# LayerNorm outputs of six token groups turned to channel rows by a DRAM write and a transposing DMA load in place of TensorE

## The chip, the cores and the metric

One core of a Trainium2 chip runs the whole program. The metric is the device time of one execution in microseconds (us), lower is better. TensorE is the matrix engine (PE, with PEld for its weight loads), VectorE is DVE, ScalarE is ACT, GpSimd is POOL, SyncE is SP. SBUF is the core's on-chip memory, in which most of the kernel's buffers lie in one piece, `arena`. PSUM is the memory that TensorE's results go to; its tiles here are `ph` (first product), `po` (second product) and `pt` (transposes). DRAM lies outside the core.

## The reference, cut to what matters

Two kinds of layer alternate, twice. A is a gated long convolution, B is a channel MLP. `x` is 2048 tokens of 512 channels, in bfloat16.

```python
x = A_q
x = x + _A_ref(_layernorm(x), A_k, A_v, ...)   # = x + layernorm(x) * y ; y depends on k and v only
x = x + _B_ref(_layernorm(x), w1, b1, w2, b2)
x = x + _A_ref(_layernorm(x), A_k, A_v, ...)   # the same y
x = x + _B_ref(_layernorm(x), w1, b1, w2, b2)

def _B_ref(x, w1, b1, w2, b2):
    y = _layernorm(x)
    h = _gelu(y @ w1 + b1)          # 512 -> 1376
    return h @ w2 + b2              # 1376 -> 512
```

The kernel computes `y` once, in its first part (up to about 118 us). The second part, the MLP part, works on groups of 512 tokens: four groups of layer 1 (numbers 0 to 3) and four of layer 2 (4 to 7). The LayerNorm of a group leaves tokens on partitions. The first matrix product needs channels on partitions, so the LayerNorm's output must be transposed: 512 x 512 elements, 512 KB, which is 16 blocks of 128 x 128.

## The kernel before: the parts that matter

```python
GT, CT, FT = 4, 4, 11       # token tiles of a group, channel tiles, hidden tiles
lnT = [place(f"lnT{i}", [P, CT, GT * P], ...) for i in range(2)]   # channel rows
lnx = [place(f"lnx{i}", [P, GT, D], ...) for i in range(2)]        # token rows

def prep(g):                           # VectorE, with a power step on GpSimd
    ln = lnx[n % 2]
    layernorm(LN[2 + n % 2], ln, g)    # x = x + layernorm(x) * y
    nc.vector.tensor_tensor(tmpa[:], ln[:], YA[...], ALU.mult)
    nc.vector.tensor_tensor(xg, xg, tmpa[:], ALU.add)
    layernorm(LN[n % 2], ln, g)        # the MLP's own LayerNorm
    return n

# PSUM: ps2 has 3 buffers for ph and 3 for po, ps3 has 2 for pt
def ln_transpose(n):                                    # TensorE, then ScalarE
    ln, lt = lnx[n % 2], lnT[n % 2]
    for i in range(GT):
        pt = ps3.tile([P, CT, P], BF16, tag="pt")
        for ct in range(CT):
            nc.tensor.transpose(pt[:, ct, :], ln[:, i, ct * P:(ct + 1) * P], IDt[:])
        nc.scalar.activation(lt[:, :, i * P:(i + 1) * P], pt[:], AF.Copy)

def mm1(n): ...    # first product, 11 x 4 matmuls into ph, gelu on ScalarE into hT
def mm2(n, g, last, between=None):                      # second product
    for i in range(GT):
        if i == GT - 1 and between is not None:
            between()                                   # the next group's transposes
        ...        # 11 matmuls into po, VectorE adds po to x; layer 2 stores x

for i, (l, g) in enumerate(seq):
    mm1(ns[i])
    nxt = None
    if 0 < i < len(seq) - 1:
        ns[i + 1] = prep(seq[i + 1][1])
        nxt = lambda n=ns[i + 1]: ln_transpose(n)
    if i == 0:
        ln_transpose(1)
    if prev is not None:
        mm2(ns[prev], seq[prev][1], seq[prev][0] == 1, nxt)
    prev = i
```

The order of the text is not the order on an engine: the program's scheduler orders each engine's instructions by what depends on what. Only the first part has a hand-written order.

## Time and profile before

| | before |
|---|---|
| time, median of 3 runs | 285.94 us (285.75 to 286.86) |
| span of the profiled run | 283.2 us (that run took 284.89 us, quicker than every other run of this kernel on record, 285.16 us and up) |
| PE, DVE, ACT, POOL busy | 93%, 66%, 59%, 13% of the span |
| mean granted TensorE clock | 0.992 |

The share of the span hides the stages, so the windows view is read first. Its columns are the window, its length, then the busy time with the count of instructions of TensorE, its weight loads, VectorE, ScalarE and GpSimd, the granted clock, the DMA engines' busy share and GB/s. This is a middle window of the MLP part of the kernel before:

```profile
150.00:170.00 20.00, 19.91 (x105) 9.51 (x104) 14.51 (x34) 9.72 (x15) 2.41 (x4) 1.00 0.00 1
```

TensorE is busy 19.91 of 20 us at full clock. ScalarE and VectorE have slack, and the DMA engines stand still. What TensorE does is what counts.

The chain of waits in order of time (start, duration, what) shows what it does in one group of the kernel before:

```profile
150.11 9.50 PE ph L611 x44
159.61 7.13 PE po L623 x33
166.74 0.24 PE pt L602 x4
167.06 0.61 ACT arena L603
167.71 0.38 PE pt L602 x4
168.09 0.22 PE po L623
168.31 0.27 PE pt L602 x4
168.58 1.73 PE po L623 x8
170.31 9.50 PE ph L611 x44
```

From one first product to the next are 170.31 − 150.11 = 20.20 us. The 44 matmuls of the first product take 9.50 us, 0.216 us each. Those of the second take as long (44 x 0.216). The remaining 1.20 us belong to the transposes (pt). A ScalarE copy (ACT arena L603, 0.61 us) stands on the chain between the transposes.

The groups view gives engine, operation, count, busy time and mean ns of one. These are the kernel before's ScalarE copies and transposes:

```profile
L603 ACT ACTIVATE arena<-pt 128x512 bf16<-128x512 bf16 x28 | 15.2, 594 | 38.4 <-PE pt L602 38.2
L602 PE MATMUL pt<-IDt,arena 128*128 128x128 bf16 x112 | 9.6, 218 | 0.5
```

Seven groups are transposed here: 7 x 16 = 112 transposes, 7 x 4 = 28 copies.

### The profile page before, as it was taken

How to read it: one execution, taken by the hardware profiler on the slowest of the kernel's cores; microseconds unless marked ns; L12 is line 12 of the kernel's file. 1: busy time of each engine (PE TensorE's matmuls, PEld its weight loads, DVE VectorE, ACT ScalarE, POOL GpSimd, SP SyncE). 2: the span in 40 equal slices, each digit the busy share in tenths (PEclk: the TensorE clock that was granted, in tenths of full speed). 3: DMA queues.
4: the chain of work that ended last, by engine and by line, in shares of the span. 5: the costliest groups of instructions: out<-in, count | busy, mean ns of one | idle time of the engine just before them, and what ended most of it. 6: DMA issues, size and time to landing. Idle time of an engine off the chain costs nothing.

```text
span 283.2 us, 5560 instructions
## 1 busy us (share of the span) xinstructions
PE 262.8 (93%) x2304; PEld 173.4 (61%) x2304; DVE 187.1 (66%) x346; ACT 167.1 (59%) x210; POOL 36.1 (13%) x67
## 2 busy tenths in 40 slices
PE   3999999999998973779999999999999999999995
PEld 3999999998997973435444444454454454444442
DVE  0989578889999999987565767767767510210221
ACT  1586646779899798887835536437247157067000
POOL 3670000000005103311101101101101100000000
PEclk9999999999999999799999999999999999999999
DMA  7993607994300380000000000000000010110111
GB/s 233 350 420 102 264 2 164 211 216 140 169 2 0 110 293 0 3 1 0 0 2 0 1 0 2 1 0 2 0 0 0 21 56 0 39 38 0 39 56 56
DMA packets 7821, 21.20 MB, mean 75 GB/s; under 512 B 1298, under 2 KB 5108, under 8 KB 6644
## 3 DMA queue, kind: packets, MB, share of 16 engines
q1 hardware_dynamic: 7042, 20.78, 23.1%
q8 instruction: 18, 0.29, 0.4%
q10 hardware_dynamic: 674, 0.07, 0.2%
q0 software_dynamic: 80, 0.00, 0.1%
q14 instruction: 7, 0.06, 0.1%
HBM read 14.56 MB, written 2.10 MB: 59 GB/s over the span
## 4 chain that ended last, share of the span: by engine, by line
PE 79%; DVE 13%; ACT 4%; issue 2%; DMA 1%; POOL 0%; ACTq 0%; DVEq 0%
PE ph L611 26%; PE po L623 26%; PE p_119 L417 3%; PE pt L602 2%; PE p_118 L340 2%; DVE lst_106 L241 2%; DVE T_96 L455 2%; PE p_119 L340 1%; DMA arena<-in_A_ssm_k_dram 1%; PE p_117 L340 1%; PE p_120 L323 1%; ACT arena L603 1%; PE p_118 L417 1%; PE p_117 L323 1%; PE p_118 L323 1%
## 5 line engine op out<-in xcount | busy, mean ns | idle before, releaser
L623 PE MATMUL po<-arena 128*128 128x512 bf16 (+1 forms) x352 | 80.7, 379 | 0.0
L611 PE MATMUL ph<-arena 128*128 128x512 bf16 (+1 forms) x352 | 78.1, 381 | 1.7 <-ACT arena L613 1.7
L613 ACT ACTIVATE arena<-ph,B_74 128x512 bf16<-128x512 f32 (+1 forms) x88 | 60.2, 687 | 26.7 <-PE ph L611 26.7
L611 PEld LDWEIGHTS <-arena 128*128 128x128 bf16 (+1 forms) x352 | 35.4, 101 | 43.1 <-issue 2.8
L626 DVE TENSOR_TENSOR arena<-po,arena 128x512 bf16<-128x512 f32 x32 | 22.0, 687 | 59.0 <-PE po L623 59.0
L623 PEld LDWEIGHTS <-arena 128*128 128x128 bf16 (+1 forms) x352 | 33.8, 98 | 37.4
L603 ACT ACTIVATE arena<-pt 128x512 bf16<-128x512 bf16 x28 | 15.2, 594 | 38.4 <-PE pt L602 38.2
L417 PEld LDWEIGHTS <-arena 128*128 128x128 bf16 x256 | 15.0, 98 | 0.2
L223 ACT ACTIVATE arena<-p_118 128x1024 bf16<-128x1024 f32 (+1 forms) x8 | 10.0, 1247 | 6.5 <-PE p_118 L377 4.7
L323 PEld LDWEIGHTS <-arena 128*128 128x128 bf16 x128 | 11.9, 99 | 1.9 <-issue 0.4
L225 DVE COPY arena<-p_117 128x2048 bf16<-128x2048 bf16 x6 | 7.3, 1220 | 8.0 <-PE p_117 L363 6.9
L489 PEld LDWEIGHTS <-GPt 128*128 128x128 bf16 x128 | 8.3, 104 | 6.4 <-issue 3.7
L602 PEld LDWEIGHTS <-arena 128*128 128x128 bf16 x112 | 8.0, 97 | 6.1 <-issue 3.6
L241 DVE BATCH_NORM_STATS2 lst_106<-arena 128x6 f32<-128x512 bf16 (+2 forms) x20 | 11.2, 578 | 0.3
L225 DVE COPY arena<-p_119 128x2048 bf16<-128x2048 bf16 (+1 forms) x9 | 10.4, 1159 | 1.0 <-PE p_119 L511 0.6
L241 DVE BATCH_NORM_STATS2 lst_110<-arena 128x6 f32<-128x512 bf16 x16 | 10.8, 687 | 0.3
L223 ACT ACTIVATE arena<-p_119 128x1024 bf16<-128x1024 f32 (+3 forms) x8 | 9.5, 1190 | 2.4 <-PE p_119 L377 1.8
L250 POOL TENSOR_TENSOR lrs_108<-lrs_108,mhalf 128x4 f32<-128x4 f32 (+1 forms) x5 | 4.8, 967 | 41.9 <-DVE lnm_109 L247 41.9
L602 PE MATMUL pt<-IDt,arena 128*128 128x128 bf16 x112 | 9.6, 218 | 0.5
L241 DVE BATCH_NORM_STATS2 lst_102<-arena 128x6 f32<-128x512 bf16 x16 | 9.9, 680 | 0.1
L241 DVE BATCH_NORM_STATS2 lst_98<-arena 128x6 f32<-128x512 bf16 x16 | 9.9, 679 | 0.1
L394 POOL TENSOR_SCALAR DG<-IDt,sF 128x128 bf16<-128x128 bf16 x16 | 9.3, 598 | 0.1
(158 smaller groups left out, 404.9 us busy)
## 6 DMA issues: line engine op xcount, KB each, us to landing
arena<-arena SPq DMA_DIRECT2D x8, 512.0 KB, 8.1
arena<-in_A_ssm_k_dram SPq DMA_DIRECT2D x4, 512.0 KB, 4.9
arena<-in_A_k_dram SPq DMA_DIRECT2D x4, 512.0 KB, 6.2
arena<-in_A_v_dram SPq DMA_DIRECT2D x2, 1024.0 KB, 9.5
arena<-tabM SPq DMA_DIRECT2D x1, 2048.0 KB, 7.6
arena<-in_A_q_dram SPq DMA_DIRECT2D x1, 2048.0 KB, 7.9
out_dram<-arena SPq DMA_DIRECT2D x16, 128.0 KB, 1.7
arena<-in_B_w_dram SPq DMA_DIRECT2D x1, 1376.0 KB
```

The costliest lines, as they stand in the source:

```text
L223: nc.scalar.activation(dst, src, AF.Copy)
L225: nc.vector.tensor_copy(dst, src)
L241: nc.vector.bn_stats(self.st[:, i, h, :], x_t[:, GT * g + i, c0:c9])
L323: nc.tensor.matmul(o[:, i, :], src[:, 4 * q + i, cs], Ft[:].rearrange("p x m -> p (x m)"), start=True, stop=True)
L340: nc.tensor.transpose(o[:, i, :], zk, IDt[:])
L417: nc.tensor.matmul(o[:, i, :], w, DG[:, cc, t, :], start=t == 0, stop=t == KS - 1)
L602: nc.tensor.transpose(pt[:, ct, :], ln[:, i, ct * P:(ct + 1) * P], IDt[:])
L603: nc.scalar.activation(lt[:, :, i * P:(i + 1) * P], pt[:], AF.Copy)
L611: nc.tensor.matmul(ph[0:m, :], W1t[:, ct, ft * P:ft * P + m], lt[:, ct, :], start=ct == 0, stop=ct == CT - 1)
L613: nc.scalar.activation(ht[0:m, ft, :], ph[0:m, :], AF.Gelu_apprx_tanh, bias=B1[0:m, ft:ft + 1])
L623: nc.tensor.matmul(po[:], ht[0:m, ft, i * P:(i + 1) * P], W2t[0:m, ft, :], start=ft == 0, stop=ft == FT - 1)
L626: nc.vector.tensor_tensor(xs, po[:], xs, ALU.add)
```

## The change

The 16 transposes and 4 copies of each of the groups 2 to 7 go. Instead GpSimd's queue writes the LayerNorm's output to DRAM, and SyncE's queue loads it back with a DMA that transposes on the way. Such a path is long, so LayerNorms are written two groups ahead, with three buffers in place of two. Group 1 keeps its TensorE transposes.

The diff is cut. Left out are the move of one scratch tile, an unused pool, and index changes.

```diff
+    dram = ctx.enter_context(tc.tile_pool(name="dram", bufs=1, space=bass.MemoryType.DRAM))
...
-    lnT = [place(f"lnT{i}", [P, CT, GT * P], (54 + 4 * i) * K) for i in range(2)]
-    lnx = [place(f"lnx{i}", [P, GT, D], (96 + 4 * i) * K) for i in range(2)]
+    lnT = [place(f"lnT{i}", [P, CT, GT * P], off * K) for i, off in enumerate((54, 58, 86))]
+    lnx = [place(f"lnx{i}", [P, GT, D], (96 + 4 * i) * K) for i in range(3)]
+    lnd = [dram.tile([GT * P, D], BF16, name=f"lnd{i}") for i in range(3)]
...
         layernorm(LN[n % 2], ln, g)
+        nc.gpsimd.dma_start(lnd[n % 3][:, :].rearrange("(i p) d -> p i d", p=P), ln[:])
+        nc.sync.dma_start_transpose(lnT[n % 3][:], lnd[n % 3][:, :])
         return n
...
-        def mm2(n, g, last, between=None):
+        def mm2(n, g, last):
...
-            nxt = None
-            if 0 < i < len(seq) - 1:
-                ns[i + 1] = prep(seq[i + 1][1])
-                nxt = lambda n=ns[i + 1]: ln_transpose(n)
+            if i < len(seq) - 2:
+                ns[i + 2] = prep(seq[i + 2][1])
```

More of the change, by code (lines that the diff above doesn't have):

```diff
@@ L148 @@
     const = ctx.enter_context(tc.tile_pool(name="const", bufs=1))
-    rot = ctx.enter_context(tc.tile_pool(name="rot", bufs=2))
+    dram = ctx.enter_context(tc.tile_pool(name="dram", bufs=1, space=bass.MemoryType.DRAM))
     ROW = 149 * K // 2
@@ L268 @@
     KSW = place("KSW", [P, 2, NA, D // 2], 64 * K)
-    lnT = [place(f"lnT{i}", [P, CT, GT * P], (54 + 4 * i) * K) for i in range(2)]
-    lnx = [place(f"lnx{i}", [P, GT, D], (96 + 4 * i) * K) for i in range(2)]
-    tmpa = place("tmpa", [P, GT, D], 104 * K)
+    lnT = [place(f"lnT{i}", [P, CT, GT * P], off * K) for i, off in enumerate((54, 58, 86))]
+    lnx = [place(f"lnx{i}", [P, GT, D], (96 + 4 * i) * K) for i in range(3)]
+    tmpa = place("tmpa", [P, GT, D], 108 * K)
+    lnd = [dram.tile([GT * P, D], BF16, name=f"lnd{i}") for i in range(3)]
     V2 = place("V2", [P, 2, NA, D // 2], 0)
@@ L285, in prep @@
         xg = x_t[:, GT * g:GT * g + GT, :]
-        ln = lnx[n % 2]
+        ln = lnx[n % 3]
         layernorm(LN[2 + n % 2], ln, g)
@@ L597, in ln_transpose @@
         def ln_transpose(n):
-            ln, lt = lnx[n % 2], lnT[n % 2]
+            ln, lt = lnx[n], lnT[n]
             for i in range(GT):
@@ L605, in mm1 @@
         def mm1(n):
-            lt, ht = lnT[n % 2], hT[n % 2]
+            lt, ht = lnT[n % 3], hT[n % 2]
             for ft in range(FT):
@@ L613, in mm1 @@
                 nc.scalar.activation(ht[0:m, ft, :], ph[0:m, :], AF.Gelu_apprx_tanh, bias=B1[0:m, ft:ft + 1])
-        def mm2(n, g, last, between=None):
+        def mm2(n, g, last):
             ht = hT[n % 2]
             for i in range(GT):
-                if i == GT - 1 and between is not None:
-                    between()
                 po = ps2.tile([P, D], F32, name="po", tag="po")
@@ L643 @@
             if prev is not None:
-                mm2(ns[prev], seq[prev][1], seq[prev][0] == 1, nxt)
+                mm2(ns[prev], seq[prev][1], seq[prev][0] == 1)
             prev = i
```

## The prediction

> **What bounds the kernel now.** The profiled span is 283.2 us (286 us timed). In its second half, from 118 us, TensorE is the limit. The windows view gives it 19.91 of every 20 us busy from 130 to 250 us at granted clock 1.00; ScalarE has 9.7 and VectorE at most 14.5 of 20. In the chain of waits a middle group is 20.20 us long (150.11, 170.31, 190.52, 210.72, 230.92, 251.12: the starts of the first matrix product): 44 matmuls of 0.216 us (9.50 us), 44 of the second product (9.50 us), and 1.20 us for the 16 transposes of the next group's LayerNorm output. The chain shows "PE pt" at 2.3% and the ScalarE copy of that PSUM tile at 1%; the first half (conv, to 118 us) is not touched.
>
> **Removed.** 96 transposes and 24 ScalarE copies (0.594 us each, 14 us in all). ScalarE has slack, so the copies are worth nothing by themselves. On the chain the gain is about 1.20 us for each of six groups: 7.2 us, 2.5% of the run. The transposes of group 1 stay.
>
> **Added.** Six 512 KB writes to DRAM from GpSimd's queue, six 512 KB transposing loads on SyncE's queue; the DMA engines are almost idle there (0 to 1 tenths from 120 us). A 128 KB store lands in 1.7 us here, a 512 KB load in 4.9 to 6.2 us. For the crossbar no duration stands in this trace. The Trainium skill, "DMA: Bandwidth & Descriptors", section "Latency and other measured facts", gives 261 GB/s with a non-contiguous middle dimension, hence an estimate of 2 us plus a fixed cost of about 2 us for 512 KB. I expect about 4 us of write and 4 to 8 us of load, 8 to 12 us in all.
>
> **Moved, and the slack.** LayerNorms already run ahead on VectorE: the second LayerNorm of group 2 ends at 128.5 us (VectorE timeline), while its product would start at 131.85 + 9.50 + 7.56 = 148.9 us. That leaves 20 us. Group 3: ends 139.7, needed 167.9, 28 us. From group 4 on the LayerNorm can start when the second product of four groups earlier is added; it takes about 13 us, and is needed two periods of 19 us later: about 25 us of slack. So all transfers should be hidden and the third buffers avoid waits for reuse. GpSimd's descriptor work may delay the next LayerNorm's power step by 1 to 2 us, which VectorE can absorb.
>
> **Sum.** 285.9 − 7.2 = 278.7 us; I add 0.2 us for small waits between VectorE's additions and the three shared PSUM buffers: 278.9 us. Range (8 in 10): 277.9 to 282.5. Faster by over 2% (under 280.3): 0.78; within 2%: 0.17; slower: 0.05.
>
> **What would show it.** Chain: the starts of the first product 19.0 to 19.1 us apart instead of 20.2; "PE pt" down to one group's 16 transposes; "ACT arena" copies x4. Groups: transposes x16. TensorE idle before the first product: none put down to a DMA. DMA issues: transposing load under 10 us to landing; write under 5 us. Tail after the last addition unchanged (3.5 us).
>
> **What would make it wrong.** (1) A slow crossbar: "VectorE: DVE Perf Modes", section "The three transpose paths", gives 1309 ns for one 128x128 block; 16 of these in series would be an estimated 21 us, longer than a 19 us period: every group would then wait for its DMA, and the kernel would be slower. (2) A scheduler order that puts VectorE's additions behind a LayerNorm waiting for GpSimd, so that PSUM buffers come free late: some tenths of a us per group. (3) The DRAM write or the transfer chain delaying output stores at the end. (4) Denser matmuls lowering the granted clock; at 19.91 of 20 busy already, I expect no change.

## The result, and the profile after

| | before | after |
|---|---|---|
| time, median of 4 runs each | 285.85 us (285.70 to 286.86) | 279.08 us (278.90 to 279.37) |
| ratio | | 0.9757 (0.9733 to 0.9781) |
| repeated in the last group of runs | 286.14 us | 278.54 us, ratio 0.9723 (0.9700 to 0.9747) |
| span of the profiled run | 283.2 us | 277.7 us |
| PE busy, ACT busy | 262.8, 167.1 us | 257.6, 153.8 us |
| mean granted TensorE clock | 0.992 | 0.988 |

A ratio is the mean time of one kernel's runs over that of the other's in the same rounds, so it is not quite the ratio of the medians. The bracket is its 95% interval. The kernel is faster by 2.4 to 2.8%.

The same window of the changed kernel, from the windows view: TensorE has no gap at all, ScalarE does 2 us less, and the DMA engines now work.

```profile
150.00:170.00 20.00, 20.00 (x95) 9.15 (x93) 15.01 (x35) 7.55 (x11) 3.23 (x5) 1.00 0.23 57
```

The chain of waits of the changed kernel, over the same two first products:

```profile
150.45 9.50 PE ph L615 x44
159.95 9.51 PE po L625 x44
169.46 9.50 PE ph L615 x44
```

The group is 19.01 us long, and no transpose, copy or DMA stands in it. The spans of the two profiled runs differ by only 5.5 us, because the first parts differ: TensorE resumes the first product of group 0 at 121.80 us before and at 123.33 us after. In the first part both kernels have the same hand-written order. The timeline of the changed kernel shows TensorE waiting 1.69 us for a load of `k` near the start, which the profiled run of the kernel before did not do. Other profiles resume group 0 at 122.25 to 123.92 us, save the slow run of e10 and the e6 with a wait of its own (both below); e9, which is the kernel before but for its transposes, does so at 123.11 us. So nothing shows that the change itself delays the first part. From here on I also give the **MLP part**: from the start of the 32 matmuls with which TensorE resumes group 0 to the start of VectorE's last addition, read from the chain (before, then after):

```profile
121.80 7.07 PE ph L611 x32
279.69 0.69 DVE arena L626
```

```profile
123.33 7.07 PE ph L615 x32
274.07 0.69 DVE arena L628
```

Before, it is 279.69 − 121.80 = 157.89 us; after, 274.07 − 123.33 = 150.74 us. It is 7.15 us shorter: 1.19 us in the first of the six intervals (18.26 to 17.07 us) and 5 x 1.19 us in the others.

The view of DMA issues (what, queue, count, KB, median us from issue to landing) shows the added work; `lnd` are the three buffers in DRAM:

```profile
lnd_115<-arena POOLq DMA_DIRECT2D x2, 512.0 KB, 3.4
lnd_113<-arena POOLq DMA_DIRECT2D x2, 512.0 KB, 4.2
lnd_114<-arena POOLq DMA_DIRECT2D x2, 512.0 KB, 3.6
arena<-lnd_115 SPq DMA_TRANSPOSE x2, 4.4
arena<-lnd_113 SPq DMA_TRANSPOSE x2, 4.2
arena<-lnd_114 SPq DMA_TRANSPOSE x2, 4.4
```

How early does the data land? Group 2 is the tightest. Three lines of the changed kernel's timeline, of VectorE, GpSimd's queue and SyncE's queue (start, duration on the engine, what):

```profile
128.62 1.38 DVE L259 TENSOR_SCALAR arena<-arena,lrs_99,lnm_100 128x512 bf16<-128x512 bf16 x4 [1.05 <-POOL lnm_100 L251]
130.30 0.89 POOL L293 DMA_DIRECT2D lnd_115<-arena  x1 [1.72 <-DVE lnm_112 L247]
133.79 1.67 SPq L294 DMA_TRANSPOSE arena<-lnd_115  x1
```

The LayerNorm ends at 130.00 us, and the load is issued at 133.79 and lands 4.4 us later, at about 138.2 us. Its product begins at 150.45 us, so 12 us are left over.

### The profile page after: what moved, and what is told of

It reads as the page before. It is cut to its first block, busy times and chain, and to the rows that moved or that the text cites. A ratio compares the mean times of both kernels' runs of the same rounds, so it can differ in the third digit from the quotient of the medians. Undisturbed runs are those within 1.5% of the kernel's fastest.

```text
span 277.7 us, 5353 instructions
## 1 busy us (share of the span) xinstructions
PE 257.6 (93%) x2208; PEld 168.6 (61%) x2208; DVE 187.0 (67%) x346; ACT 153.8 (55%) x186; POOL 41.1 (15%) x73
## 4 chain that ended last, share of the span: by engine, by line
PE 76%; DVE 13%; DMA 5%; ACT 2%; issue 2%; ACTq 0%; POOL 0%; DVEq 0%
PE po L625 27%; PE ph L615 26%; DMA sT<-in_A_shift_k_dram 3%; PE p_121 L421 3%; DMA arena<-in_A_k_dram 2%; PE p_120 L344 2%; DVE lst_105 L241 2%; DVE T_95 L459 2%; PE p_121 L344 1%; PE p_119 L344 1%; PE p_120 L421 1%; PE p_122 L327 1%; PE p_122 L344 1%; DVE arena L535 1%; DVE arena L427 1%
## 5 line engine op out<-in xcount | busy, mean ns | idle before, releaser
L615 PE MATMUL ph<-arena 128*128 128x512 bf16 (+1 forms) x352 | 79.1, 385 | 1.1 <-ACT arena L617 1.1
L625 PE MATMUL po<-arena 128*128 128x512 bf16 (+1 forms) x352 | 77.7, 379 | 0.0
L615 PEld LDWEIGHTS <-arena 128*128 128x128 bf16 (+1 forms) x352 | 35.6, 101 | 43.3 <-issue 3.6
L625 PEld LDWEIGHTS <-arena 128*128 128x128 bf16 (+1 forms) x352 | 34.3, 98 | 40.9
L421 PEld LDWEIGHTS <-arena 128*128 128x128 bf16 x256 | 15.0, 98 | 0.2
L327 PEld LDWEIGHTS <-arena 128*128 128x128 bf16 x128 | 11.9, 99 | 1.9 <-issue 0.4
L225 DVE COPY arena<-p_119 128x2048 bf16<-128x2048 bf16 x6 | 7.3, 1221 | 7.8 <-PE p_119 L367 6.7
L225 DVE COPY arena<-p_120 128x2048 bf16<-128x2048 bf16 x7 | 8.6, 1221 | 3.0 <-PE p_120 L405 2.0
L596 POOL MEMSET arena<- 1x512 bf16 x2 | 1.0, 519 | 61.5 <-PE p_122 L448 61.5
L250 POOL TENSOR_TENSOR lrs_103<-lrs_103,mhalf 128x4 f32<-128x4 f32 x4 | 5.0, 1246 | 26.8 <-DVE lnm_104 L247 26.8
```

The costliest lines, as they stand in the source:

```text
L225: nc.vector.tensor_copy(dst, src)
L250: nc.gpsimd.tensor_tensor(self.rs[:, a:b], self.rs[:, a:b], mhalf[:, a:b], ALU.pow)
L327: nc.tensor.matmul(o[:, i, :], src[:, 4 * q + i, cs], Ft[:].rearrange("p x m -> p (x m)"), start=True, stop=True)
L421: nc.tensor.matmul(o[:, i, :], w, DG[:, cc, t, :], start=t == 0, stop=t == KS - 1)
L615: nc.tensor.matmul(ph[0:m, :], W1t[:, ct, ft * P:ft * P + m], lt[:, ct, :], start=ct == 0, stop=ct == CT - 1)
L625: nc.tensor.matmul(po[:], ht[0:m, ft, i * P:(i + 1) * P], W2t[0:m, ft, :], start=ft == 0, stop=ft == FT - 1)
```

## The experiments

The theory: TensorE is the limit of the MLP part, the change takes six groups' transposes off it, and the transfers are hidden in slack. The rivals: the gain is the deeper lookahead; or the relief of ScalarE; or the transfers are only just hidden, and the lookahead is needed for that.

| run | median us | ratio to before (95%) | MLP part us |
|---|---|---|---|
| before | 285.8 to 286.1 | 1 | 157.89 |
| after, repeated (e0) | 278.54 | 0.9723 (0.9700 to 0.9747) | 150.74 |
| e1 TensorE transposes, two ahead | 285.62 | 0.9992 (0.9966 to 1.0018) | 157.53 |
| e2 DMA, one ahead, two buffers | 278.86 | 0.9756 (0.9734 to 0.9778) | 150.74 |
| e3 after + waste transposes | 284.40 | 0.9953 (0.9926 to 0.9979) | 156.09 |
| e4 after + waste copies, badly placed | 281.90 | 0.9861 (0.9839 to 0.9884) | 153.88 |
| e4b after + waste copies, in place | 278.62 | 0.9738 (0.9712 to 0.9764) | 150.74 |
| e9 before, transposes in pairs | 284.28 | 0.9938 (0.9911 to 0.9964) | 156.30 |
| e8 two hops more | 278.30 | 0.9730 (0.9703 to 0.9756) | 150.74 |
| e8 four hops more | 286.93 | 1.0018 (0.9981 to 1.0055) | 159.41 |
| e6 group 1 too | 279.09 | 0.9764 (0.9726 to 0.9802) | 149.69 |
| e7 SBUF to SBUF | 278.86 | 0.9736 (0.9712 to 0.9760) | 150.74 |
| e10 SBUF to SBUF, group 1 too | 278.57 | 0.9729 (0.9692 to 0.9767) | 149.69 |

Every run's output was correct. Waste instructions write what nobody reads.

### e1: the lookahead alone

```diff
 # from the changed kernel
-        nc.gpsimd.dma_start(lnd[n % 3]..., ln[:])
-        nc.sync.dma_start_transpose(lnT[n % 3][:], lnd[n % 3][:, :])
 # and mm2(..., between) with ln_transpose(n) put back, on three buffers
```

> LayerNorms two groups ahead and three buffers, but the transposes of groups 2 to 7 stay on TensorE with their ScalarE copies. Theory (the gain is TensorE time taken off the chain): no gain, 285 to 286.5 us, groups 20.1 to 20.3 us apart. Rival (the gain is the deeper lookahead): 279 to 281 us.

Measured: 285.62 us, ratio 0.9992. The groups are 20.14 us apart. The deeper lookahead by itself is worth nothing that these runs show.

### e2: the DMA alone, one group ahead with two buffers

```diff
-    lnT ... (54, 58, 86) ; lnx, lnd ... range(3) ; n % 3
+    lnT ... (54, 58)     ; lnx, lnd ... range(2) ; n % 2
-            if i < len(seq) - 2:
-                ns[i + 2] = prep(seq[i + 2][1])
+            if 0 < i < len(seq) - 1:
+                ns[i + 1] = prep(seq[i + 1][1])
```

> DMA transposes, but written one group ahead and with two buffers, as before the change. Theory: the LayerNorms run as early as their data allows whatever the text's order, so the transfers (about 9 us from the LayerNorm's end to landing, out of 20 to 25 us of slack) stay hidden: 278.5 to 279.8 us. Rival (the two-groups-ahead part is needed to hide the transfers): waits of several us before each first product, 282 us or more.

Measured: 278.86 us, with an MLP part of 150.74 us, that of the changed kernel to the hundredth. "Two groups ahead" and the third buffers are not needed. The scheduler already lets the LayerNorms run as soon as their data is there, and two buffers are enough for that.

### e3: the transposes alone

```diff
+        def pe_only(n):                      # called where ln_transpose stood
+            ln = lnx[n % 3]
+            for i in range(GT):
+                pt = ps3.tile([P, CT, P], BF16, name="pt", tag="pt")
+                for ct in range(CT):
+                    nc.tensor.transpose(pt[:, ct, :], ln[:, i, ct * P:(ct + 1) * P], IDt[:])
```

> The changed kernel with the 96 TensorE transposes put back into their old places as waste (nobody reads them), no ScalarE copies. Theory: the whole loss comes back, 279.1 + 6 x 1.1 = 285.7 us (285 to 286.5). Rival (ScalarE's copies, or the waits for them, were the cost): stays at 279 to 280.5 us.

Measured: 284.40 us, below the expected range. The MLP part gets 5.35 us back of the 7.15. The chain of waits of this run shows a whole group's transposes in one piece:

```profile
167.17 0.90 PE pt L614 x16
```

Sixteen transposes that wait for nobody take 0.90 us, not 1.20. So about 0.30 us per group were something else. The ScalarE copy on the chain of the kernel before (ACT arena L603, 0.61 us) suggests what: `pt` has two PSUM buffers and four tiles, so TensorE waits until ScalarE has emptied one. e9 tests this.

### e9: the kernel before, without that wait

```diff
 # from the kernel before
-            for i in range(GT):
-                pt = ps3.tile([P, CT, P], BF16, name="pt", tag="pt")
+            for i in range(0, GT, 2):
+                pt = ps3.tile([P, CT, 2, P], BF16, name="pt", tag="pt")   # one bank, two token tiles
 ...         # 8 transposes, then one ScalarE copy of 128x1024
```

> The kernel before, with the transposes of two token tiles in one PSUM bank and one ScalarE copy for both, so that all 16 transposes of a group fit the two banks and never wait for a copy. Theory (of the 1.20 us per group, 0.90 us is the transposes themselves and 0.30 us TensorE waiting for ScalarE to empty one of two PSUM buffers): 285.8 - 7 x 0.3 = 283.8 us (283.4 to 284.8). Rival (the transposes alone take 1.20 us, or their weight loads do): 285.2 to 286.5 us.

Measured: 284.28 us, inside the range. The chain of waits of this run:

```profile
167.95 0.90 PE pt L603 x16
168.85 0.86 PE po L624 x4
171.23 9.50 PE ph L612 x44
187.86 0.90 PE pt L603 x16
191.13 9.50 PE ph L612 x44
```

With all four token tiles in the two banks, the 16 transposes take 0.90 us in the real kernel too, and a group is 191.13 − 171.23 = 19.90 us long. So 1.20 us = 0.90 us of transposes + 0.30 us of waiting for ScalarE's copies. The new path removes both, and with e3 the sum closes: 5.35 + 6 x 0.30 = 7.15 us.

In the windows view this wait is hardly seen (0.09 us idle of 20), since the record of a matmul of the second product lasts 379 ns, longer than the 216 ns to the start of the next. The starts show it. The timeline of the kernel before:

```profile
166.58 0.61 PE L602 MATMUL pt<-IDt,arena 128*128 128x128 bf16 x8
167.03 0.59 PE L623 MATMUL po<-arena 128*128 128x512 bf16 x2
167.71 0.38 PE L602 MATMUL pt<-IDt,arena 128*128 128x128 bf16 x4
```

After two matmuls of 0.216 us from 167.03 us on, the next could start at 167.46. It starts at 167.71 us, just after the first copy's end at 167.67: 0.25 us of the 0.30. The rest lies before the last four transposes. This small edit of the kernel before gains 0.6% without any DMA.

### e4 and e4b: the copies alone

```diff
+        def act_only(n):                     # e4: called where ln_transpose stood
+            for i in range(GT):
+                nc.scalar.activation(junk[:, i, :], lnx[n % 3][:, i, :], AF.Copy)
 # e4b: the source is x_t[:, GT * g + 2, :], which the third addition of that second product has just written
```

> The changed kernel with 24 ScalarE copies of 128x512 bf16 put back as waste, no TensorE transposes. Theory: no change, 278.6 to 279.8 us. Rival (ScalarE relief is the gain): 284 us or more.

e4 measured 281.90 us, outside the range. The copies' source is the LayerNorm's output, so for group 3 the scheduler placed copies among the gelu activations of group 1's first product. ScalarE's timeline in e4:

```profile
138.34 0.69 ACT L622 ACTIVATE arena<-ph,B 128x512 bf16<-128x512 f32 x1 [0.18 <-PE ph L620]
141.14 0.63 ACT L612 ACTIVATE arena<-arena 128x512 bf16<-128x512 bf16 x1 [2.12 <-DVE arena L259]
141.68 0.67 ACT L622 ACTIVATE arena<-ph,B 128x512 bf16<-128x512 f32 x1
```

ScalarE stood 2.12 us for a LayerNorm that was not finished, and the gelu behind that copy started only at 141.68 us, where the gelus before it had come every 0.86 us. So `ph` buffers stayed full and TensorE stood 1.51 us for that gelu (its timeline, at 142.40 us). Group 2's waste copies did the like earlier: group 1's real copies came late behind them, and TensorE stood 1.19 us (at 132.25 us). These two stands are 2.70 of the 3.14 us by which the MLP part is longer. It is a flaw of the experiment: from 152.95 us on, the groups are 19.01 us apart, copies and all. e4b puts the copies where the real ones stood.

> The waste copies on ScalarE again, 24 of 128x512 bf16, but now in the place where the real ones stood (during the second product, after its third addition), not between the activations of the first product where the first try put those of groups 2 and 3. Theory (copies cost nothing where ScalarE is idle): 278.6 to 279.8 us, groups 19.0 us apart. Rival (the copies themselves cost): 281 us or more.

e4b measured 278.62 us with an MLP part of 150.74 us, and its 24 copies have 13.1 us of ScalarE's time. So ScalarE's time is worth nothing here; only a wait in the wrong place costs.

### e8: how much slack the transfers have

```diff
         nc.gpsimd.dma_start(lnd[n % 3]..., ln[:])
+        hop = lnd[n % 3]
+        for j in range(2):                  # 4 in the second run
+            nc.sync.dma_start(lnh[n % 3][j][:, :], hop[:, :])     # DRAM to DRAM, 512 KB
+            hop = lnh[n % 3][j]
-        nc.sync.dma_start_transpose(lnT[n % 3][:], lnd[n % 3][:, :])
+        nc.sync.dma_start_transpose(lnT[n % 3][:], hop[:, :])
```

> The changed kernel with two more DRAM to DRAM copies of 512 KB between the write and the transposing load, one after the other, about 4 us each (estimate from the 3.4 us write): landing about 17 us after the LayerNorm's end in place of 9. Theory (20 us of slack for group 2, 25 us for the others): still hidden, 278.6 to 280 us. Rival (the transfers are barely hidden): 282 us or more.

Two hops measured 278.30 us, just below the range, MLP part 150.74 us. A hop takes 3.9 to 4.0 us (view of DMA issues). Group 2's load is issued at 141.40 us and lands about 4.4 us later, at 145.8; its product begins at 150.11 us. Nothing is lost with the path twice as long.

> The same with four more copies: about 25 us from the LayerNorm's end to landing, and the SyncE queue held about 21 us per group, longer than a 19 us group. Theory: group 2 waits about 5 us, and the later ones some us each: 284 to 300 us, first products released by a DMA. If it stays at 279 us, the slack was larger than I computed, or a copy is faster than 4 us.

Four hops measured 286.93 us: the whole gain is gone. Its profile fell on the slowest of the four runs (288.63 us; the others 285.93 to 287.30), and there the MLP part is 8.67 us longer than that of the changed kernel. TensorE's timeline of this run shows three first products released by the DMA:

```profile
155.27 2.31 PE L620 MATMUL ph<-arena 128*128 128x512 bf16 x5 [4.24 <-DMA arena<-lnh]
157.81 9.74 PE L620 MATMUL ph<-arena 128*128 128x512 bf16 x38 [0.22 <-issue]
215.60 9.67 PE L620 MATMUL ph<-arena 128*128 128x512 bf16 x44 [0.52 <-DMA arena<-lnh]
254.60 9.67 PE L620 MATMUL ph<-arena 128*128 128x512 bf16 x43 [0.80 <-DMA arena<-lnh]
```

The waits add up to 4.24 + 0.52 + 0.80 = 5.56 us. The first of them costs more than itself: the product after it takes 167.55 − 155.27 = 12.28 us in the chain, where it takes 9.50 elsewhere. The windows view of this run shows why. The last three columns are granted clock, DMA share and GB/s:

```profile
157.00:158.00 1.00, 0.78 (x3) 0.41 (x3) 0.98 (x1) 0.69 (x1) 0.00 (x0) 0.50 0.00 0
159.00:160.00 1.00, 1.00 (x4) 0.36 (x3) 1.00 (x2) 0.65 (x1) 0.00 (x0) 0.50 0.19 66
160.60:160.80 0.20, 0.20 (x2) 0.10 (x1) 0.20 (x3) 0.13 (x1) 0.00 (x0) 1.00 0.00 0
```

When TensorE starts again after 4.24 us of standing still the granted clock is half, and it stays so until about 160.6 us. The Trainium skill, "TensorE: Matmul & The Clock Gate", section "Part 1: The HAM clock gate (the "warmup" mystery)", says that the clock falls to half after an idle window of about 3.4 us. This trace agrees in part: the wait of 4.24 us brought the clock down, and the waits of 0.52 and 0.80 us did not. But in steps of 0.2 us the windows view has the clock at half from 153.8 us on, when TensorE had stood for about 2.7 us (since 151.03 us). Waits and slow clock together, 5.56 + 2.78 = 8.34 us, account for nearly all of the 8.67.

This brackets the slack. For group 2 the path from the LayerNorm's end to landing may grow from about 8 us by 8 us, and not by 16, as 20 us of slack say.

### e7, e6 and e10: a shorter path, and group 1 too

```diff
 # e7: straight from SBUF to SBUF, no DRAM, four DMAs of 128 KB per group
+        for i in range(GT):
+            nc.sync.dma_start_transpose(lnT[n % 3][:, :, i * P:(i + 1) * P], ln[:, i, :])
 # e6: group 1 as well, by DRAM, in two halves; e10: group 1 as well, straight
-            if i == 0:
-                ln_transpose(1)
```

> The changed kernel again, as the measure for the three runs beside it: 278.6 to 279.6 us.

> Transposing DMAs straight from SBUF to SBUF, four of 128 KB per group, no DRAM write and no DMA from GpSimd. Theory (all of the transfer is hidden, so a shorter one gains nothing): within 0.5 us of the changed kernel, 278.6 to 279.6 us. If these DMAs disturb TensorE or are far slower (over 4 us each), 280 us or more.

e0 measured 278.54 us, just below its range. e7 measured 278.86 us, and both have an MLP part of 150.74 us. A DMA of 128 KB straight from SBUF to SBUF lands in 2.4 us (median of 24). Since all of the transfer was hidden, a shorter one gains nothing. It does do without the DRAM buffers, the DRAM traffic and GpSimd's DMA issues, at the same time.

> The changed kernel with group 1 turned by DMA as well, in two halves of 256 KB. Theory: the last 16 transposes (1.04 us of TensorE) go too; group 1's LayerNorm ends at about 121 us and its product could begin at 130.4 us, just room for about 9 us of transfer; with the second product of group 0 to fill a short wait: 277.6 to 278.6 us, about 1 us under the changed kernel. If the transfers land late, a wait of 1 to 3 us eats the gain: 278.6 to 280.5 us.

> Both: SBUF to SBUF transposing DMAs, and group 1 turned by them too. Theory: as for the two-half version, 277.6 to 278.6 us, and less at risk of a late landing if the four short DMAs land within about 6 us.

In both traces the MLP part is 149.69 us, 1.05 us shorter, and the two first products run on without a break ("PE ph L615 x76" in the chain). That is the gain that I expected, and the transfers land in time. The whole times do not show it, and e6 misses its range for a timely landing (277.6 to 278.6 us): e6 has a median of 279.09 us (278.07 to 281.52), e10 one of 278.57 us (277.68 to 281.09), beside 278.54 us (278.26 to 278.58). For e6 its chain of waits shows a cause:

```profile
117.85 0.69 POOL lrs L250
118.56 0.83 POOL lnd L638
119.42 1.32 POOL lnm L251
120.76 1.52 ACT arena L257 x2
```

GpSimd issues the DMA of group 1's first half between two steps of the LayerNorm of its second half. The path from the end of "POOL lrs" to ScalarE's step is 120.76 − 118.54 = 2.22 us; in e0 it is 118.68 − 118.38 = 0.30 us. These 1.92 us come before the first product, where nothing hides them, and they eat the 1.05 us. e10 issues nothing from GpSimd and does not have this wait. Its profile fell on its slowest run (281.09 us), in which TensorE resumes only at 126.05 us, after waits for loads near the start (2.43 us of them in one piece, for `k`) and a stretch of half clock from about 17.5 to 20.9 us (windows view). In the three best of its six runs it took 277.68 to 277.86 us. Whether the slow three are the scatter of the first loads, as the one profile suggests, or come from the edit, these runs do not settle. So I name no version that beats the changed kernel; e10 is a candidate that would need more runs.

## Why the prediction was right

- **What bounds the kernel.** Right. TensorE is the limit of the MLP part: giving back transposes gives back time (e3), giving back 13.1 us of ScalarE work in place does not (e4b).
- **The gain, 1.20 us for each of six groups, 7.2 us.** Right: 7.15 us in the MLP part of the two profiles, with groups 19.01 us apart as predicted (19.0 to 19.1). The number held because it was read from the chain as what a group loses, whatever that consists of. What it is made of was told too simply. The prediction put 1.20 us down to "the 16 transposes" and called the copies worth nothing by themselves. As work they are (e4b), but 0.30 us of the 1.20 were TensorE waiting for them at two PSUM buffers; the transposes are 0.90 us (e3, e9).
- **The cost of the path.** Right: predicted about 4 us of write and 4 to 8 us of load, measured 3.4 to 4.2 and 4.2 to 4.4 us. The estimate rested on the 261 GB/s that the Trainium skill gives in "DMA: Bandwidth & Descriptors", section "Latency and other measured facts", plus an assumed 2 us; 4.3 us for 512 KB agrees with that sum. The feared case, 16 blocks one after the other at the 1309 ns that "VectorE: DVE Perf Modes" gives for one, about 21 us, did not occur.
- **The slack.** Right: 20 us for group 2 were predicted. The profile after gives 150.45 − 130.00 = 20.45 us, and e8 brackets it. The absolute times for group 2 were about 1.5 us later than predicted, because the profile of before fell on a run with a quick start.
- **GpSimd delaying a LayerNorm's power step.** Seen once and absorbed: VectorE waited 2.41 us instead of 1.33 for group 3's first LayerNorm. The 0.2 us that I added for small waits are not in the trace; the MLP part has none.
- **"The third buffers avoid waits for reuse".** Not needed: e2 has the same MLP part with two. This part of the change is neutral.
- **The granted clock.** Right as to the MLP part: 1.00 in both middle windows.
- **The total.** 278.9 us predicted, 279.08 and 278.54 us measured. That the first came within 0.2 us is partly luck: the two medians lie 6.77 us apart in the first rounds and 7.60 us in the last, about the 7.15 us of the MLP part.

## What to carry to other kernels

Where the profile shows one engine busy almost without gaps at full clock, as here, read the gain of moving work off it from the chain: it is what the distance between two like events loses when that work goes. The place to move it to may be slow, so long as the slack, from data ready to data needed, is longer than the path. e8 shows how sharply that turns, from free to the loss of the whole gain within two hops of 4 us. Take apart what the chain charges to an operation before replacing it: a quarter of it here was a wait for PSUM buffers, which a change of tile shape removes alone (e9). A waste-work experiment must put the waste where the real work stood, for its waits cost time here and its work did not (e4, e4b).

## What the Trainium skill lacked or had wrong

- "VectorE: DVE Perf Modes", section "The three transpose paths": 1309 ns for a 128x128 block by DMA cannot be multiplied by the number of blocks. One transposing load of 512 KB (16 blocks) from DRAM lands 4.2 to 4.4 us after its issue, little later than a plain DRAM to DRAM copy of the same size (3.9 to 4.0 us with two hops); 128 KB (4 blocks) straight from SBUF to SBUF lands in 2.4 us.
- The same table's 390 ns for a block on TensorE: it is no measure for blocks in a row. For 16 in a row the traces of e3 and e9 give 0.90 us, 56 ns per block, at a granted clock of 1.00; the record of one lasts 218 ns.
- "TensorE: Matmul & The Clock Gate", section "Part 1: The HAM clock gate (the "warmup" mystery)": the clock is said to fall after an idle window of about 3.4 us. In the run with four hops it was half after TensorE had stood for about 2.7 us. Full clock is said to return after about 3.4 us of sustained work. There it took from 155.27 to about 160.6 us, 5.3 us, with one break of 0.22 us in between. The section says that its window runs freely, so the longer return need not contradict it; one such wait does not settle it.
- "DMA: Bandwidth & Descriptors": no figure for how long a DMA issued from GpSimd holds up GpSimd's own compute. Here one of 512 KB takes 0.80 to 0.89 us of it (0.72 and 0.83 us for 256 KB in e6), and in e6 the small multiplication behind it took 1.32 us where it takes 0.20 elsewhere. Why the multiplication was slow was not tested.
